# Attention, soft mixture of experts and MLP in one kernel: the dispatch sums spread behind the dispatch products, and a new order of the tail's steps

## The chip, the cores and the metric

One core of a Trainium2 chip runs the whole program. The metric is the time of one execution on the device in microseconds (us); the median of several executions is compared. The engines are named as in the profile: PE (matrix products; PEld is its loading of the stationary operand), DVE (vector), ACT (activations and copies), POOL (general), SP (issues the DMAs; SPq is its queue).

## The reference

Three layers follow each other, in float32. Eight batches with 8 heads, 576 rows and head size 64; keys and values are averaged over groups of 8 rows, so that each row attends to 72 pooled keys:

```python
k_p = k.reshape(B, H, Sp, pool, D).mean(axis=3); v_p = ...
attn = softmax(scale * q @ k_p.T); x = attn @ v_p          # 4608 x 512
logits = x @ phi                                           # 4608 x 32 slots (8 experts x 4)
d = exp(logits - logits.max(0)); d /= d.sum(0) + 1e-9
slot_input = d.T @ x                                       # dispatch
slot_out[e] = relu(slot_input[e] @ w1[e]) @ w2[e]
c = exp(logits - logits.max(1)); c /= c.sum(1) + 1e-9
x = c @ slot_out                                           # combine
out = (s * relu(x @ w_in) ** 2 + b) @ w_out
```

The maximum and the sum of d run over all 4608 rows, for each of the 32 slots. The kernel takes them batch by batch and merges the eight results.

## The kernel before

**The loop.** `for t in range(NT + 2)` goes over 36 tiles of 128 rows; a pair of batches (pr) has 9 tiles. A table (LOOP, FIRST) says in which order the steps of the pipeline are issued in each turn. For tile t: A transposes q (PE, L353; copied by ACT, L355), B forms the scores (PE, L383; DVE takes maximum and difference, L390 and L393), C takes the exponential on ACT (L397), its sum and reciprocal on DVE (L401 to L404) and the product P on POOL (L421), D transposes P (PE, L434 and L435; ACT copies to PT, L440 and L441), E forms the logits transposed (PE, L457 and L464; ACT copies to LT, L469), F turns them back (PE, L480) and DVE adds four partial sums into L (L482). "r" takes one step of each running dispatch, "p" one step of the preparation of a next pair (kv_transpose L264 and others).

**A dispatch.** When F has done the last tile of batch b_, a generator `dispatch(b_)` is started; each `next` issues the instructions up to its next `yield`. Its steps, in order: maximum of L over the rows (md, L538); the maximum over the partitions by a transposition on PE and a DVE reduction (L545, L547); its spreading over the partitions by a product (L550) with a DVE copy into m_all (L551); the difference dd (DVE, L554); its exponential (ACT, L556); then

- zd, the sum of dd over j (DVE, L559), its sum over the partitions spread to all partitions by a product with ones (PE, L563), and the copy of that into z_all (ACT, L564);
- the dispatch products of dd with the tiles P (PE, L572 and L577) into two banks, copied by ACT to `at` (L581);
- sums of four blocks by products with sel4 (PE, L591), copied to `a` (ACT L595; for the last batch DVE L597, multiplied by m_all);
- products with the pooled values vps (PE, L601), copied by DVE into si_all (L611); for the last batch DVE adds si_sum and writes the slot inputs siz (L613).

Batches 0 to 5 (b_ < B - 2) are dispatched inside the loop, with a `yield` between zd and L563. Batches 6 and 7 are dispatched in the tail.

**The tail.** The string TAIL (L21) is a list of steps that are issued in that order after the loop: F, E, C, D for one of the last five tiles, "6" and "7" one step of the dispatch of batch 6 or 7, "m" one step of merge_1 (maximum, si and z of the first six batches: L496 to L498, then L501 and L502, then L504 to L508), M2 (L515 to L517), M3 (L521 to L526) and M4 (L531, L532) the merging with batches 6 and 7, W products that have no use but to be run, X0 to X2 the closing of a tile pool and `extra`, which opens new slots for weights in its place and lets SP issue loads into them. "G4" is D for the last tile with its two copies on DVE in place of ACT.

**After the tail.** The weights w1 and w2 come as 32 loads of 1 MB, each into a slot (tiles ring, raw, x, and one called brief). PE multiplies them in a fixed order (L933 for w1, L941 for w2); after each, its slot is free and `pump` issues the next load in the list, in order, on the SP queue. The fifth load used, `brief`, can only be issued when the tail's pools are closed (actx.close()); the load behind it in the queue is the first of w_in, which needs a slot of `raw`, and so the sixth product's end. Beside these products the DVE and ACT steps of `combine` run, and PE transposes (L892) their results. From about 285 us on (L1067) the last layer runs on PE.

**Banks.** All products other than the scores use `bank()`, one pool of four tiles in rotation (ps_w): whoever asks for a tile waits until the one that was asked for four requests earlier has been read.

Of the kernel before, what the change touches and what calls it, by code (L numbers as in the profile page):

```python
# [14 lines left out]
ALU = mybir.AluOpType  # L15
AX = mybir.AxisListType
# [1 line left out]

OPS = "o0 a0 o0 a1 b0 b1 h0 g0 o1 h1 o1 g1"
WIPOS, WOPOS = 22, 25  # L20
TAIL = "F0 6 C4 X0 D2 6 X1 E2 6 m 6 6 F2 D3 G4 6 m E4 F4 X2 7 W3 7 W2 7 7 7 6 6 7 6 m M2 M3 7 7 M4 7"  # L21
BUSY = (2, 0)
CUT = 1

# [32 lines left out]
def kernel(  # L57
# [14 lines left out]
    nc = tc.nc  # L72
    B, H, SEQ, D = q.shape
    KP = SEQ // 8
    NPR = B // 2
    E, DM, F = w1.shape
# [12 lines left out]
    one = cpool.tile([128, 1], F32, name="one")  # L89
# [6 lines left out]
    z_all = cpool.tile([128, B, 32], F32, name="z_all")  # L96
# [81 lines left out]
    W1, W2 = ([[(w, e, hf) for e in range(EG * g, EG * g + EG) for hf in range(2)] for g in range(2)] for w in ("w1", "w2"))  # L178
# [36 lines left out]
    def bank():  # L215
        return ps_w.tile([128, 512], F32, tag="w", name="w")
# [206 lines left out]
    def place(t):  # L423


        jj = t % 9
        return (0, True) if jj == 0 else ((jj - 1) % 2, jj % 2 == 0)

    def st_D(t, copy=nc.scalar.copy):
        Pf = P_t[t].rearrange("p h k -> p (h k)")  # L430
        x, last = place(t)
        pa, pb = bank(), bank()
        for c in range(4):
            nc.tensor.transpose(out=pa[:, 128 * c:128 * c + 128], in_=Pf[:, 128 * c:128 * c + 128], identity=ident)  # L434
        nc.tensor.transpose(out=pb[0:64, 0:128], in_=Pf[:, 512:576], identity=ident)  # L435
        if x == 0:
            PT_t[t // 9] = apc.tile([128, 5, 256], F32, tag="PT", name="PT", bufs=2)
        PT = PT_t[t // 9]
        r = slice(128 * x, 128 * x + 128)
        copy(out=PT[:, 0:4, r], in_=pa.rearrange("p (c x) -> p c x", c=4))  # L440
        copy(out=PT[0:64, 4, r], in_=pb[0:64, 0:128])  # L441
        if last:
            PT2_t[t] = PT

# [89 lines left out]
    def dispatch(b_):  # L534
        pr, bb = divmod(b_, 2)
        Lb = L_t[pr][:, 6 * bb:6 * bb + 5, :]
        md = ap2.tile([128, 32], F32, tag="md", name="md")
        nc.vector.tensor_reduce(out=md, in_=Lb.rearrange("p j s -> p s j"), axis=AX.X, op=ALU.max)  # L538
        yield
        if b_ < B - 2:  # L540
            yield


        ps = bank()
        nc.tensor.transpose(out=ps[0:32, 0:128], in_=md, identity=ident)  # L545
        mc = md[0:32, 0:1]
        nc.vector.tensor_reduce(out=mc, in_=ps[0:32, 0:128], axis=AX.X, op=ALU.max)  # L547
        yield
        ps = bank()
        nc.tensor.matmul(out=ps[:, 0:32], lhsT=mc.to_broadcast([32, 128]), rhs=ident[0:32, 0:32], start=True, stop=True)  # L550
        nc.vector.tensor_copy(out=m_all[:, b_, :], in_=ps[:, 0:32])  # L551
        yield
        dd = ap2.tile([128, 5, 32], F32, tag="dd", name="dd")
        nc.vector.tensor_tensor(out=dd, in0=Lb, in1=m_all[:, b_, :].unsqueeze(1).to_broadcast([128, 5, 32]), op=ALU.subtract)  # L554
        yield
        nc.scalar.activation(out=dd, in_=dd, func=ACTF.Exp)  # L556
        yield
        zd = ap2.tile([128, 32], F32, tag="zd", name="zd")
        nc.vector.tensor_reduce(out=zd, in_=dd.rearrange("p j s -> p s j"), axis=AX.X, op=ALU.add)  # L559
        if b_ < B - 2:  # L560
            yield
        ps = bank()
        nc.tensor.matmul(out=ps[:, 0:32], lhsT=one.to_broadcast([128, 128]), rhs=zd, start=True, stop=True)  # L563
        nc.scalar.copy(out=z_all[:, b_, :], in_=ps[:, 0:32])  # L564
        t0 = 9 * pr + 1 + 4 * bb
        pure = [(dd[:, (1 if bb == 0 else 0) + j, :], P_t[t0 + j]) for j in range(4)]
        dl, Pm = dd[:, 0 if bb == 0 else 4, :], P_t[9 * pr]
        at = ap2.tile([128, PQ], F32, tag="at", name="at", bufs=1)
        pss = [bank(), bank()]
        for x in range(2):  # L570
            for g, (dj, P) in enumerate(pure):
                nc.tensor.matmul(  # L572
                    out=pss[x][32 * g:32 * g + 32, 0:288], lhsT=dj, rhs=P[:, 4 * x:4 * x + 4, :], start=True, stop=False
                )

            for g in range(4):
                nc.tensor.matmul(  # L577
                    out=pss[x][32 * g:32 * g + 32, 72 * g:72 * g + 72], lhsT=dl, rhs=Pm[:, 4 * x + g, :], start=False, stop=True
                )
        for x in range(2):  # L580
            nc.scalar.copy(out=at[:, 288 * x:288 * x + 288], in_=pss[x][:, 0:288])  # L581
        yield
        if b_ >= B - 2:
            yield
        for j in range(4):
            P_t.pop(t0 + j)
        if bb == 1:
            P_t.pop(9 * pr)
        ps = bank()
        for h in range(8):  # L590
            nc.tensor.matmul(out=ps[0:72, 32 * h:32 * h + 32], lhsT=at[:, 72 * h:72 * h + 72], rhs=sel4, start=True, stop=True)  # L591
        a = ap2.tile([72, 8, 32], F32, tag="a", name="a", bufs=1)
        av = ps[0:72, 0:256].rearrange("p (h s) -> p h s", h=8)
        if b_ < B - 1:
            nc.scalar.copy(out=a, in_=av)  # L595
        else:
            nc.vector.tensor_tensor(out=a, in0=av, in1=m_all[0:72, b_].unsqueeze(1).to_broadcast([72, 8, 32]), op=ALU.mult)  # L597
        yield
        ps = bank()
        for hp in range(4):  # L600
            nc.tensor.matmul(  # L601
                out=ps[:, 64 * hp:64 * hp + 64],
                lhsT=vps_t[pr][:, 4 * bb + hp, :],
                rhs=a[:, 2 * hp:2 * hp + 2, :],
                start=True, stop=True,
            )
        pv = ps[:, 0:256].rearrange("p (c t s) -> p c t s", c=4, t=2)
        for h2 in range(2):
            r = slice(64 * h2, 64 * h2 + 64)
            if b_ < B - 1:  # L610
                nc.vector.tensor_copy(out=si_all[r, b_], in_=pv[r, :, h2, :])  # L611
            else:
                nc.vector.tensor_tensor(  # L613
                    out=siz[r].rearrange("p (e r) -> p e r", r=132)[:, :, 0:128].rearrange("p e (c s) -> p e c s", s=32)[:, :, :, 0:4],
                    in0=pv[r, :, h2, :].rearrange("p c (e j) -> p e c j", j=4),
                    in1=si_sum[r].rearrange("p c (e j) -> p e c j", j=4),
                    op=ALU.add,
                )
# [119 lines left out]
    n0 = NT - 5  # L738

    def warm(n):  # L740
        ps = bank()
        for _ in range(n):
            nc.tensor.matmul(out=ps[:, 0:128], lhsT=ident, rhs=ident, start=True, stop=True)

    def step(gen, n=1):
        for _ in range(n):
            next(gen, None)
# [4 lines left out]
    cmb = [combine(pr) for pr in range(NPR)]  # L752
    siz = None
    for op in TAIL.split():
        if op[0] in "FECDG":
            t = n0 + int(op[1])
            if op[0] == "G":
                st_D(t, nc.vector.tensor_copy)
            else:
                {"F": st_F, "E": st_E, "C": st_C, "D": st_D}[op[0]](t)  # L760
        elif op[0] == "M":
            (merge_2, merge_3, merge_4)[int(op[1]) - 2]()
        elif op[0] == "W":
            warm(int(op[1:]))
        elif op[0] == "c":
            step(cmb[int(op[1])])
        elif op[0] == "X":
            (bctx, sctx, cctx)[int(op[1])].close()
            x_ = extra(XR[1 + int(op[1])], op[1] == "2")
            siz = siz if x_ is None else x_  # L770
        else:
            step(gens[op])
# [151 lines left out]
    for n_, key in enumerate(EORD):  # L924
# [3 lines left out]
        if w_ == "w1":  # L928
            for n in range(2):
                for c in range(2):  # L930
# [3 lines left out]
                        out=l1[g][n][32 * cg:32 * cg + 32, :],  # L934
                        lhsT=siz[:, 128 * e + 32 * kc:128 * e + 32 * kc + 32],
                        rhs=w[:, c, 512 * n:512 * n + 512],
                        start=(ge == 0), stop=(ge == EG - 1),
                    )
        else:
            for c in range(4):  # L940
                nc.tensor.matmul(  # L941
                    out=so_ps[32 * c:32 * c + 32, :],
                    lhsT=h1z[:, 4 * hf + c, 36 * ge + 16 - 4 * e:36 * ge + 48 - 4 * e],
                    rhs=w[:, c, :],
                    start=(e == 0 and hf == 0), stop=(e == E - 1 and hf == 1),
# [167 lines left out]
    for g, n in enumerate(GROUPS[:-1]):  # L1113
        m = GROUPS[g + 1]
# [9 lines left out]
    for i in range(len(steps)):  # L1124
# [18 lines left out]
        if t_wi:  # L1143
            f = min(t_wi)
            ps = ps_h.tile([128, 2, 512], F32, tag="h", name="h")
# [4 lines left out]
        if g == len(GROUPS) - 1:  # L1150
            if blk == 0 and fi == 0:

                ps = ps_h.tile([128, 2, 512], F32, tag="h", name="bias_ps")
# [5 lines left out]
            while bias:  # L1159
                p = part_of(*bias.popleft())  # L1160
# [31 lines left out]
```

## Time and profile before

| what | value |
|---|---|
| runs shown, median | 731.09 us (729.94 to 734.69, 3 runs) |
| profiled execution, its own time | 734.33 us |
| its span, first to last instruction | 732.2 us |
| PE busy | 662.1 us, 90% |
| DVE busy | 501.9 us, 69% |
| ACT busy | 412.0 us, 56% |
| POOL busy | 297.1 us, 41% |
| mean granted clock of PE | 0.960 of full |

Read: the profiled execution was slower than the median of the runs by 3.2 us, and its span leaves 2.1 us around it. A busy share is a mean over stages. Up to about 204 us the loop runs, from 204 to 228 us the tail, from 228 to 285 us the weights of the experts and the start of the last layer, and from there to the end PE is busy almost without a break.

### The profile page before, as it was taken

The page shows a single profiled execution, that of the slowest core. Times are in us where ns is not written, and L with a number is a line of the kernel's source. Part 1 is how long each engine was busy: PE and PEld are TensorE (multiplying, and loading weights), DVE is VectorE, ACT ScalarE, POOL GpSimd, SP SyncE. Part 2 cuts the span into 40 slices and gives each one's busy share as a digit, 9 for nine tenths or more (in the row PEclk, how much of TensorE's full clock was granted, in tenths as well). Part 3 has the DMA queues.
Part 4 walks back from the last instruction along what each step waited for, and adds up shares of the span by engine and source line. Part 5 has one row for each costly group of instructions (what it writes and reads, how often), then busy time and mean ns, then how long its engine had stood idle before and what let it go on. Part 6 is the DMA issues. An engine that isn't in the chain of part 4 may idle for free.

```text
span 732.2 us, 11203 instructions
## 1 busy us (share of the span) xinstructions
PE 662.1 (90%) x4294; PEld 517.9 (71%) x4294; DVE 501.9 (69%) x806; ACT 412.0 (56%) x713; POOL 297.1 (41%) x221
## 2 busy tenths in 40 slices
PE   4676879788877987999999999999999999999997
PEld 3565757577653325778888887878888888888885
DVE  6869778657667268788767687889655766456543
ACT  3454656466431435778665666666666666555552
POOL 3647556533210025356322443346331433799100
PEclk9886999999997998999999999999999999999999
DMA  8996455444384993101111011031100000123322
GB/s 298 375 328 209 174 168 181 172 173 164 125 288 175 379 358 123 58 0 58 59 57 59 8 61 48 1 115 59 58 1 0 1 1 1 44 95 95 100 100 87
DMA packets 41317, 88.87 MB, mean 121 GB/s; under 512 B 6960, under 2 KB 15152, under 8 KB 41264
## 3 DMA queue, kind: packets, MB, share of 16 engines
q1 hardware_dynamic: 41264, 88.16, 34.6%
q8 instruction: 34, 0.56, 0.3%
q14 instruction: 19, 0.16, 0.1%
HBM read 78.71 MB, written 9.44 MB: 120 GB/s over the span
## 4 chain that ended last, share of the span: by engine, by line
PE 75%; DVE 15%; ACT 4%; POOL 2%; issue 2%; DMA 1%; SPq 1%; DVEq 0%; ACTq 0%; POOLq 0%
PE o L1067 52%; PE h L1010 4%; PE sc L383 2%; PE l L933 2%; DVE sm L401 2%; DVE S L393 2%; PE so_ps L941 2%; DVE mx L390 2%; PE w L572 2%; PE w L434 1%; DMA ring<-in_v_dram 1%; ACT S L397 1%; PE w L591 1%; PE w L457 1%; PE ct L892 1%
## 5 line engine op out<-in xcount | busy, mean ns | idle before, releaser
L1067 PE MATMUL o<-whi,gh 128*128 128x512 f32 x576 | 229.1, 398 | 2.5 <-DVE gh L1037 2.5
L1067 PE MATMUL o<-whi,gl 128*128 128x512 f32 x576 | 225.2, 392 | 1.0 <-DVE gl L1038 1.0
L1067 PE MATMUL o<-wlo,gh 128*128 128x512 f32 x576 | 225.2, 391 | 0.0
L1019 ACT ACTIVATE r<-h 128x768 f32<-128x768 f32 x95 | 77.3, 813 | 151.8 <-PE h L1010 148.0
L1038 DVE TENSOR_TENSOR gl<-r,gh 128x768 fp32r<-128x768 f32 (+1 forms) x97 | 114.4, 1181 | 63.3 <-ACT gh L1027 62.9
L1080 DVE SCALAR_TENSOR_TENSOR part<-o,sb_t,part 128x512 f32<-128x512 f32 x144 | 99.6, 743 | 50.4 <-PE o L1067 47.8
L1067 PEld LDWEIGHTS o<-wlo,gh 128*128 128x128 f32 x576 | 108.5, 188 | 24.0
L1067 PEld LDWEIGHTS o<-whi,gh 128*128 128x128 f32 x576 | 108.4, 188 | 23.8 <-issue 5.6
L1067 PEld LDWEIGHTS o<-whi,gl 128*128 128x128 f32 x576 | 108.6, 189 | 21.7 <-DVE gl L1038 3.1
L825 POOL TENSOR_TENSOR fr<-fr,xp 128x512 f32<-128x512 f32 x28 | 41.1, 1467 | 182.4 <-ACT fr L824 160.3
L1020 ACT ACTIVATE r<-r 128x768 f32<-128x768 f32 x95 | 80.5, 847 | 3.0
L1027 ACT CAST gh<-r 128x768 fp32r<-128x768 f32 x95 | 79.4, 836 | 2.4
L421 POOL TENSOR_TENSOR P<-S,rs 128x576 f32<-128x576 f32 x32 | 37.3, 1166 | 89.7 <-DVE rs L404 54.9
L1161 POOL TENSOR_TENSOR part<-part,wsum 128x512 f32<-128x512 f32 x36 | 53.3, 1518 | 10.5 <-ACT wsum L1155 10.5
L1010 PE MATMUL h<-cT,S 128*128 128x384 f32 x192 | 48.8, 336 | 0.5 <-DVE S L853 0.5
L826 POOL TENSOR_TENSOR th<-th,fr 128x512 f32<-128x512 f32 x28 | 43.0, 1537 | 2.2
L383 PE MATMUL sc<-kb,qT 128*128 128x144 f32 x256 | 42.0, 313 | 0.0
L1010 PEld LDWEIGHTS h<-cT,S 128*128 128x128 f32 x192 | 35.9, 188 | 8.1 <-DVE S L853 0.7
L401 DVE TENSOR_REDUCE sm<-S 128x8 f32<-128x576 f32 x36 | 27.0, 750 | 21.2 <-ACT S L397 21.0
L390 DVE TENSOR_REDUCE mx<-sc 128x8 f32<-128x576 f32 x36 | 26.4, 732 | 18.7 <-PE sc L383 15.3
L383 PEld LDWEIGHTS sc<-kb,qT 128*128 128x128 f32 x256 | 37.8, 212 | 0.4 <-ACT qT L355 0.2
L397 ACT ACTIVATE S<-S 128x576 f32<-128x576 f32 x36 | 24.6, 682 | 22.1 <-DVE S L393 22.0
(212 smaller groups left out, 913.1 us busy)
## 6 DMA issues: line engine op xcount, KB each, us to landing
ring<-in_moe_w_dram SPq DMA_DIRECT2D x14, 1024.0 KB, 7.3
x<-in_moe_w_dram SPq DMA_DIRECT2D x13, 1024.0 KB, 10.5
raw<-in_moe_w_in_dram SPq DMA_DIRECT2D x8, 1024.0 KB, 5.5
raw<-in_moe_w_out_dram SPq DMA_DIRECT2D x8, 1024.0 KB, 4.8
out_dram<-part SPq DMA_DIRECT2D x32, 256.0 KB, 2.5
ring<-in_q_dram SPq DMA_DIRECT2D x7, 1024.0 KB, 9.5
ring<-in_v_dram SPq DMA_DIRECT2D x9, 768.0 KB, 10.0
ring<-in_k_dram SPq DMA_DIRECT2D x7, 768.0 KB, 7.0
```

The lines of the kernel that those rows point to most:

```text
L383: nc.tensor.matmul(out=sc[:, i // 2, 2 * KP * (i % 2):2 * KP * (i % 2) + 2 * KP], lhsT=qT[:, i, :], rhs=kb[:, H * bb + 4 * (j % 2) + i, :] ...
L401: nc.vector.tensor_reduce(out=sm, in_=S, axis=AX.X, op=ALU.add)
L825: nc.gpsimd.tensor_tensor(out=fr, in0=fr, in1=xp, op=ALU.mult)
L826: nc.gpsimd.tensor_tensor(out=th if dst is None else dst, in0=th, in1=fr, op=ALU.add)
L1010: nc.tensor.matmul(out=h[x][:, 0:384] if i == 0 else h[:, x, 0:384], lhsT=Sw_t[f], rhs=cT(c, 384), start=True, stop=True)
L1019: nc.scalar.activation(out=r, in_=h[:, :, 0:384], func=ACTF.Relu)
L1020: nc.scalar.activation(out=r, in_=r, func=ACTF.Square)
L1027: nc.scalar.copy(out=gh_t[i], in_=r)
L1038: nc.vector.tensor_tensor(out=gl[:, x], in0=r[:, x], in1=gh[:, x].bitcast(F32), op=ALU.subtract)
L1067: nc.tensor.matmul(out=o_t[tt], lhsT=l[:, x, 128 * c:128 * c + 128], rhs=r, start=(fi == 0 and n == 0), stop=(fi == GROUPS[g] - 1 and n == 2),
L1080: nc.vector.scalar_tensor_tensor(out=p, in0=o_t[tt], scalar=sb_t[:, 0:1], in1=p, op0=ALU.mult, op1=ALU.add)
L1161: nc.gpsimd.tensor_tensor(out=p, in0=p, in1=wsum, op=ALU.add)
```

## The change

In `dispatch`, the sum over the partitions (product L563 and its copy L564) is taken out of the place in front of the dispatch products and put behind them. For batches 0 to 5 zd stays in its own step and the spreading comes one step later, at the head of the step that begins with the sel4 products. For batches 6 and 7 zd, too, moves behind the dispatch products, into the step that did nothing before; for batch 7 the copy is made by DVE. The string TAIL is new: D for the last tile makes its copies on ACT (D4 in place of G4, whose code goes), the last step of merge_1 stands before F4, M2 directly behind the exponential of batch 7, and M3 before the last step of batch 6.

```diff
-TAIL = "F0 6 C4 X0 D2 6 X1 E2 6 m 6 6 F2 D3 G4 6 m E4 F4 X2 7 W3 7 W2 7 7 7 6 6 7 6 m M2 M3 7 7 M4 7"
+TAIL = "F0 6 C4 X0 D2 6 X1 E2 6 m 6 6 F2 D3 m D4 6 E4 6 m F4 X2 7 W3 7 W2 7 7 7 M2 6 7 7 M3 6 7 M4 7"
...
         zd = ap2.tile([128, 32], F32, tag="zd", name="zd")
-        nc.vector.tensor_reduce(out=zd, in_=dd.rearrange("p j s -> p s j"), axis=AX.X, op=ALU.add)
+
+        def z_sum():
+            nc.vector.tensor_reduce(out=zd, in_=dd.rearrange("p j s -> p s j"), axis=AX.X, op=ALU.add)
+
+        def z_spread(copy):
+            ps = bank()
+            nc.tensor.matmul(out=ps[:, 0:32], lhsT=one.to_broadcast([128, 128]), rhs=zd, start=True, stop=True)
+            copy(out=z_all[:, b_, :], in_=ps[:, 0:32])
+
         if b_ < B - 2:
+            z_sum()
             yield
-        ps = bank()
-        nc.tensor.matmul(out=ps[:, 0:32], lhsT=one.to_broadcast([128, 128]), rhs=zd, start=True, stop=True)
-        nc.scalar.copy(out=z_all[:, b_, :], in_=ps[:, 0:32])
         t0 = 9 * pr + 1 + 4 * bb
...
             nc.scalar.copy(out=at[:, 288 * x:288 * x + 288], in_=pss[x][:, 0:288])
         yield
-        if b_ >= B - 2:
+        if b_ < B - 2:
+            z_spread(nc.scalar.copy)
+        else:
+            z_sum()
+            z_spread(nc.scalar.copy if b_ < B - 1 else nc.vector.tensor_copy)
             yield
```

On PE, inside the loop at the dispatch of batch 1, before: the product with ones (zd, one) stands between the scores and the dispatch products (P, dd).

```order
L383 MATMUL sc<-kb_124,qT 128x144 x4
L563 MATMUL w<-zd,one 128x32
L572 MATMUL w<-P_2_104,dd 32x288 x2
L572 MATMUL w<-P_3_105,dd 32x288 x2
L577 MATMUL w<-Pm,dd 32x72 x4
L572 MATMUL w<-P_2_104,dd 32x288 x2
L572 MATMUL w<-P_3_105,dd 32x288 x2
L577 MATMUL w<-Pm,dd 32x72 x4
L353 MATMUL w<-ident,qm 128x128 x4
```

The same place on PE now, from the end of the dispatch products (here L583) on: the product with ones (now L565) stands behind the steps A, E and D and in front of the products with sel4 (now L601).

```order
L583 MATMUL w<-Pm,dd 32x72 x4
L353 MATMUL w<-ident,qm 128x128 x4
L457 MATMUL w<-PT,vpf 32x256 x4
L464 MATMUL w<-PT,vpf 32x64 x4
L434 MATMUL w<-ident,P_0_102 128x128 x4
L435 MATMUL w<-ident,P_0_102 64x128
L565 MATMUL w<-zd,one 128x32
L601 MATMUL w<-sel_62,at 72x32 x8
L383 MATMUL sc<-kb_124,qT 128x144 x4
```

So the dispatch products come directly behind the scores, and PE has four other steps before it asks for zd.

On DVE, at the end of the tail, before: what stands between the copies of batch 6 into si_all and the multiplication `a` of batch 7 (L597), namely the last step of merge_1 (L504 to L508), M2 and M3.

```order
L611 COPY si_all<-w 64x128 x2
L504 TENSOR_TENSOR z_all<-z_all,m_all 128x192
L506 TENSOR_REDUCE zt<-z_all 128x32
L507 COPY z_all<-zt 128x32
L508 COPY m_all<-mt 128x32
L515 TENSOR_REDUCE mt<-m_all 128x32
L516 TENSOR_TENSOR m_all<-m_all,mt 128x96
L521 TENSOR_TENSOR z_all<-z_all,m_all 128x96
L523 TENSOR_REDUCE zt<-z_all 128x32
L524 TENSOR_SCALAR zt<-zt 128x32
L525 RECIPROCAL zt<-zt 128x32
L526 TENSOR_TENSOR m_all<-m_all,zt 128x96
```

The same place on DVE now, from the difference dd of batch 7 on to the multiplication `a` (now L607):

```order
L554 TENSOR_TENSOR dd<-L_75,m_all 128x160
L515 TENSOR_REDUCE mt<-m_all 128x32
L516 TENSOR_TENSOR m_all<-m_all,mt 128x96
L561 TENSOR_REDUCE zd<-dd 128x32
L566 COPY z_all<-w 128x32
L521 TENSOR_TENSOR z_all<-z_all,m_all 128x96
L523 TENSOR_REDUCE zt<-z_all 128x32
L524 TENSOR_SCALAR zt<-zt 128x32
L525 RECIPROCAL zt<-zt 128x32
L526 TENSOR_TENSOR m_all<-m_all,zt 128x96
L621 COPY si_all<-w 64x128 x2
L607 TENSOR_TENSOR a<-w,m_all 72x256
```

M2 has moved ahead of zd, the step L504 to L508 is gone from here (it now stands before F4), and the copies into si_all follow M3.

## Rows read from the trace of the kernel before

**Rows 1.** Waits of PE from 75 to 204 us: total, times, longest.
```profile
PE w L563 <- DVE zd L559: 9.3, 4, 3.0
```

**Rows 2.** Timeline of PE, L563: start, duration, ..., [idle before <- releaser]; batches 1, 2, 4, 5.
```profile
104.84 0.61 PE L563 MATMUL w<-zd,one 128*128 128x32 f32 x2 [3.00 <-DVE zd L559]
131.63 0.45 PE L563 MATMUL w<-zd,one 128*128 128x32 f32 x2 [2.35 <-DVE zd L559]
177.61 0.38 PE L563 MATMUL w<-zd,one 128*128 128x32 f32 x2 [1.31 <-DVE zd L559]
195.37 0.38 PE L563 MATMUL w<-zd,one 128*128 128x32 f32 x2 [2.60 <-DVE zd L559]
```

**Rows 3.** Timeline of ACT: exponentials and copies of batches 1 and 5, and in the tail.
```profile
102.27 0.34 ACT L556 ACTIVATE dd<-dd 128x160 f32<-128x160 f32 x1 [2.03 <-DVE dd L554]
103.20 0.59 ACT L440 COPY PT<-w 128x512 f32<-128x512 f32 x1
192.80 0.34 ACT L556 ACTIVATE dd<-dd 128x160 f32<-128x160 f32 x1 [1.09 <-DVE dd L554]
211.31 0.19 ACT L564 COPY z_all<-w 128x32 f32<-128x32 f32 x1 [2.04 <-PE w L563]
```

**Rows 4.** Busy time by stretch: length, PE, PEld, DVE, ACT, POOL, granted clock, DMA share, GB/s.
```profile
104.00:108.00 4.00, 3.16 (x35) 1.80 (x36) 2.08 (x5) 1.08 (x4) 3.11 (x3) 0.57 0.95 302
132.00:135.00 3.00, 3.00 (x35) 1.52 (x34) 0.91 (x2) 0.88 (x3) 1.93 (x2) 0.50 0.63 239
196.70:200.00 3.30, 3.30 (x40) 2.05 (x29) 1.18 (x4) 1.89 (x5) 0.18 (x1) 0.50 0.00 0
224.00:234.00 10.00, 7.59 (x36) 3.35 (x40) 8.00 (x25) 1.33 (x3) 0.00 (x0) 0.50 0.43 154
```

**Rows 5.** Timeline of PE in the tail and behind it.
```profile
210.90 0.38 PE L563 MATMUL w<-zd,one 128*128 128x32 f32 x2 [1.18 <-DVE zd L559]
217.88 0.41 PE L563 MATMUL w<-zd,one 128*128 128x32 f32 x2 [0.31 <-DVE zd L559]
218.22 0.69 PE L572 MATMUL w<-P,dd 128*32 128x288 f32 x8
219.58 1.10 PE L601 MATMUL w<-a,vps 72*128 72x64 f32 x8
225.46 1.97 PE L601 MATMUL w<-a,vps 72*128 72x64 f32 x8 [3.77 <-DVE a L597]
228.37 4.49 PE L933 MATMUL l<-ring,siz 128*32 128x512 f32 x20 [0.94 <-DVE siz L613]
...
234.69 1.04 PE L933 MATMUL l<-brief,siz 128*32 128x512 f32 x8
```

**Rows 6.** Timeline of DVE at the tail's end.
```profile
221.32 0.36 DVE L504 TENSOR_TENSOR z_all<-z_all,m_all 128x192 f32<-128x192 f32 x1
...
223.43 0.26 DVE L521 TENSOR_TENSOR z_all<-z_all,m_all 128x96 f32<-128x96 f32 x1 [0.35 <-ACT m_all L517]
...
224.99 0.42 DVE L597 TENSOR_TENSOR a<-w,m_all 72x256 f32<-72x256 f32 x1
```

**Rows 7.** Timeline of the SP queue, loads of weights.
```profile
214.80 1.51 SPq L136 DMA_DIRECT2D x<-in_moe_w_dram  x1
216.35 0.89 SPq L136 DMA_DIRECT2D x<-in_moe_w_dram  x1
...
227.50 0.37 SPq L136 DMA_DIRECT2D brief<-in_moe_w_dram  x1
236.67 0.37 SPq L136 DMA_DIRECT2D raw<-in_moe_w_in_dram  x1
```

**Rows 8.** These two x loads and the brief load: size, us from issue to landing.
```profile
x<-in_moe_w_dram SPq DMA_DIRECT2D x1, 1024.0 KB, 10.5
x<-in_moe_w_dram SPq DMA_DIRECT2D x1, 1024.0 KB, 11.4
...
brief<-in_moe_w_dram SPq DMA_DIRECT2D x1, 1024.0 KB, 4.8
```

More of the change, by code (lines that the diff above doesn't have):

```diff
@@ L427, in place, with st_D @@
         return (0, True) if jj == 0 else ((jj - 1) % 2, jj % 2 == 0)
-    def st_D(t, copy=nc.scalar.copy):
+    def st_D(t):
         Pf = P_t[t].rearrange("p h k -> p (h k)")
@@ L439, in st_D @@
         r = slice(128 * x, 128 * x + 128)
-        copy(out=PT[:, 0:4, r], in_=pa.rearrange("p (c x) -> p c x", c=4))
-        copy(out=PT[0:64, 4, r], in_=pb[0:64, 0:128])
+        nc.scalar.copy(out=PT[:, 0:4, r], in_=pa.rearrange("p (c x) -> p c x", c=4))
+        nc.scalar.copy(out=PT[0:64, 4, r], in_=pb[0:64, 0:128])
         if last:
@@ L754 @@
     for op in TAIL.split():
[L755 to L760, printed above, removed]
+        if op[0] in "FECD":
+            {"F": st_F, "E": st_E, "C": st_C, "D": st_D}[op[0]](n0 + int(op[1]))
         elif op[0] == "M":
```

## The prediction

> **What bounds the kernel now.** I read the waits of PE first, then the timelines of PE and ACT around them, then the chain from the tail into the weights. The reader is to see three things.
>
> In the loop PE stands still in front of one instruction, the product with ones (L563). It waits 9.3 us in four stretches for zd [rows 1], those of batches 1, 2, 4 and 5: 3.00, 2.35, 1.31 and 2.60 us [rows 2]; batches 0 and 3 show none. Behind it on PE the dispatch products are queued, and they don't read zd; they read dd, whose exponential ended earlier: at batch 1 at 102.27 + 0.34 = 102.61, while PE came free at 104.84 - 3.00 = 101.84 and zd let it go at 104.84 [rows 2, 3]. DVE makes zd only after the sums of the next tile. So the wait is one of order, not of data. Nothing in the loop runs against an outer clock that I can find, so a time won there is kept until another engine stands in the way.
>
> In the tail PE waits for zd again, 1.18 us for batch 6 and 0.31 for batch 7, and then 3.77 us for `a` of batch 7 [rows 5], because DVE does the rest of merge_1, M2 and M3 between the copies of batch 6 and that multiplication: from 221.32 to 224.99 [rows 6]. During that idle time the granted clock falls to 0.50, the 1.2 GHz level, and it is there from 224 to 234 [rows 4]. The last products (L601) take 1.97 us, the same kind before them 1.10 [rows 5].
>
> Behind the tail, the weights of w1 and w2 are multiplied, and new loads are issued as slots come free. `brief` is issued at 227.50, when the tail's last products are over, and the next load only at 236.67, after the sixth weight is used [rows 7]. From there on loads and products follow one another at a pace that the start decides, and the last layer follows on them. I take it that a shift at `brief` is a shift of the end.
>
> **The change part by part.** *Loop, dispatch products ahead of the product with ones.* At batch 1 the wait is 3.00; the products must still wait for the exponential, 102.61 - 101.84 = 0.77. Their second bank was asked for last by D, whose copy to PT ends at 103.20 + 0.59 = 103.79 [rows 3]; the products take 1.36 us in the tail (218.22 to 219.58 [rows 5]), so the first half would be through at about 103.3, and another 0.5 is waited. That leaves 3.00 - 0.77 - 0.5 = 1.7. At batches 2 and 4 I count the whole wait, 2.35 and 1.31. At batch 5 the exponential ends at 192.80 + 0.34 = 193.14 against 195.37 - 2.60 = 192.77 [rows 2, 3], so 2.60 - 0.37 = 2.2. The sum is 1.7 + 2.35 + 1.3 + 2.2 = 7.6 us (rounded up). The product itself (0.38 to 0.61 us [rows 2]) is not saved, it comes back in front of the products with sel4; there zd has long been made, so it waits for nothing. Behind it on PE the sel4 products and the next scores are queued; their delay is the same 0.4 us that the dispatch products are spared.
>
> The loop's term has bounds. Above: PE ran at half clock behind three of these waits: 3.16 us of PE work at 0.57 after batch 1, 3.00 at 0.50 after batch 2, 3.30 at 0.50 after batch 5 [rows 4]. With the waits gone that work could run at the full 2.4 GHz, worth 3.16 x 0.43 + 3.00 / 2 + 3.30 / 2 = 4.5 us more, 12.1 in all. Below: another engine may be late next; then I count only the 1.7 of batch 1. I take 7.6, the value of the waits' own rows, and leave the clock out, since PE keeps other waits.
>
> *Tail, up to the first weight.* For batch 6 PE no longer waits for zd: 1.2 us. The copies of the last D go from DVE to ACT, where 2.04 us were idle before 211.31 [rows 3]; two such copies are 0.85 at most, judged by 0.59 for the larger, so they are covered; without that cover they would cost that 0.85. For batch 7 wait and product stood ahead of the dispatch products, 218.22 - 217.57 = 0.65, as the wait of 0.31 began at 217.57 [rows 5]. Then the main piece: from the end of the dispatch products, about 219.58, to `a` at 224.99 there were 5.4 us [rows 5, 6]. Now there stand the product with ones (0.3), its copy (0.2, as ACT's), M3 (224.99 - 223.43 = 1.56 [rows 6]) and the two copies into si_all (from 220.68, where the products L601 end, to 221.32 [rows 5, 6], 0.64): 2.7. M2 and the end of merge_1 lie beside PE's work earlier, where DVE is waiting. That saves 2.7. Products with sel4 for batch 7 end near the same moment and don't bind. With PE's wait gone, the last L601 should take 1.10 in place of 1.97: 0.9. Sum 1.2 + 0.65 + 2.7 + 0.9 = 5.4 us at the first weight product, so 228.37 becomes 223.0, and the issue of `brief` 222.1, counted in the time of before.
>
> *Tail, up to brief.* The first weights now run at the full clock: four of them at 1.04 us each (as the one of `brief` [rows 5]) are through at 227.1, where before they took until 234.69 [rows 5]. But `brief` is not there yet. It stands in the queue behind x loads that land at 214.80 + 10.5 = 225.3 and 216.35 + 11.4 = 227.75 [rows 7, 8]. That load rate doesn't depend on the change. At their spacing of 2.45 us `brief` lands at 230.2. PE waits some 3 us for it, a new wait that replaces the one removed. The gain at that point, and from there to the end, is 234.69 - 230.2 = 4.5 us. Bounds: it lands with the load ahead of it, 227.75 (gain 6.9), or it takes the whole 4.8 us that it took alone [rows 8] behind it, 232.55 (gain 2.1). I take 4.5, the value from the two queued loads, because it is queued as they are.
>
> The sum: 7.6 + 4.5 = 12.1 us. The profiled execution took 734.33, so its like would take 722.2. That execution was 3.2 above the median of the runs; against the median of 731.09 the forecast is 719.0.
>
> **The rivals.** *The clock comes back.* As above, three half-clock stretches stand right behind removed waits [rows 4]; if all go, the gain is 12.1 + 4.5 = 16.6, and the time 731.09 - 16.6 = 714.5. Against it: the new wait at `brief`, and waits in the loop that stay. The Trainium skill, "TensorE: Matmul & The Clock Gate", section "HAM oscillation — how this bites in real kernels", says that a kernel whose products are short bursts between waits keeps falling back to the low clock and pays for it each time; by that rule the loop's falls would go with their waits, and a new one could come at `brief`. By that rule, the trace agrees as far as [rows 4] go, where each of the three stretches stands behind a wait for zd.
>
> *Another engine is late in the loop.* The removed wait is replaced by the next one, as DVE's sums and POOL's products follow one another too. For it: at batch 1 PT's copy at 103.79 is 1.95 behind PE's free moment. Then the loop gives 1.7 and the sum is 1.7 + 4.5 = 6.2: 724.9.
>
> *Brief lands late.* If it needs the full 4.8 us behind the last x load, the tail gives 2.1 and the sum is 7.6 + 2.1 = 9.7: 721.4.
>
> *Slower.* Place: the banks of the dispatch products. They are asked for earlier, when ACT has not read the tiles that hold them, and ACT now has a copy for D more and is served in order. Price: each dispatch waits for ACT what it waited for DVE before. The point from which it decides is (7.6 + 4.5) / 8 = 1.5 us per dispatch; at 2.0 us in each of eight the kernel loses 16.0 - 12.1 = 3.9: 735.0. For it speaks the same PT copy, against it that only batch 1 shows it so late and that ACT is the least busy of the three engines here.
>
> **How the numbers follow.** Forecast 0.54, clock back 0.18, another engine 0.15, brief late 0.10, slower 0.03. A measurement of this kernel can tell about 1% from no change, 7.3 us, that is below 723.8 or above 738.4; 735.0 is still within 1%, but such waits would not stop at 2.0 exactly, and I give 0.02 of its 0.03 to slower. Faster: nearly all of the forecast (0.52), the clock (0.18), most of brief late (0.09) and a little of the third (0.03), together 0.82. Slower 0.02, the rest, 0.16, within 1%. The range goes from both upper bounds, 731.09 - 12.1 - 6.9 = 712.1, to both lower ones, 1.7 + 2.1 = 3.8 us and so 727.3; I give it as 712.0 to 727.0.
>
> **What would show it.** Right: PE's waits for zd are gone in the loop, the dispatch products follow the exponential or their bank; the tail from the exponential of batch 7 to the first weight is some 4 us shorter; PE has a wait of up to 3 us for `brief`; the stretch from the loop's start to the tail's is 7 to 12 us shorter, and the last layer as long as before. Wrong in the loop: waits of the same size in front of the scores, the transpositions of D or DVE's sums. Wrong in the tail: PE still waits for `a`, or the load behind `brief` is issued less than 2 us earlier, counted from the tail's start.

## The result and the profile after

| what | before | changed |
|---|---|---|
| runs beside each other, median | 730.67 us (729.94 to 734.69, 4 runs) | 722.06 us (719.37 to 727.48, 4 runs) |
| ratio | | 0.9876, 95% interval 0.9837 to 0.9915 |
| profiled execution, its own time | 734.33 us | 724.16 us |
| its span | 732.2 us | 722.0 us |
| mean granted clock of PE | 0.960 | 0.956 |

The change was run in two more series of six (e3_all and e6_change below): 0.9866 and 0.9859. A gain in us is given, here and below, as the ratio gives it: 1 less the ratio, times the median of the kernel before. One slow execution (733.7 us, in e1_loop) is in the median shown there and not in the ratio. So the change saves 9 to 10 us (9.1, 9.8 and 10.3) of the 12.1 forecast.

The waits of PE from 75 to 204 us of the changed kernel (total, times, longest), which answer to [rows 1]:

```profile
PE w L578 <- ACT dd L556: 1.3, 2, 0.9
...
PE w L601 <- ACT LT L469: 1.2, 2, 0.8
...
PE w L434 <- POOL P L421: 0.6, 1, 0.6
PE w L565 <- DVE L L482: 0.5, 1, 0.5
...
PE w L578 <- ACT PT L440: 0.3, 1, 0.3
```

zd, 9.3 us before, is gone from the list. L578 are now the dispatch products, L565 the product with ones, L601 the products with sel4. The timeline of PE at batches 1, 2 and 5, which answers to [rows 2]:

```profile
103.63 0.69 PE L578 MATMUL w<-P,dd 128*32 128x288 f32 x8 [0.88 <-ACT dd L556]
...
104.76 0.69 PE L578 MATMUL w<-P,dd 128*32 128x288 f32 x8 [0.31 <-ACT PT L440]
...
107.51 0.31 PE L565 MATMUL w<-zd,one 128*128 128x32 f32 x2
108.19 1.23 PE L601 MATMUL w<-sel,at 128*72 128x32 f32 x16 [0.37 <-ACT LT L469]
...
131.44 0.41 PE L565 MATMUL w<-zd,one 128*128 128x32 f32 x2 [0.51 <-DVE L L482]
131.98 1.80 PE L601 MATMUL w<-sel,at 128*72 128x32 f32 x16
...
192.41 1.23 PE L601 MATMUL w<-sel,at 128*72 128x32 f32 x16 [0.79 <-ACT LT L469]
193.47 1.92 PE L383 MATMUL sc<-kb,qT 128*128 128x144 f32 x8
```

The dispatch products at batch 1 wait for the exponential and then for D's copy to PT, as foreseen. What is new are small waits: one of D's transpositions (L434) for POOL's P, 0.6 us, and those of L565 and L601, which name neither zd nor `at`. L565 doesn't read L, nor L601 LT; counted by the rotation of four, L565 of batch 2 asks for the bank of F, which F's sum (L482) is still reading, and L601 for the bank of E, which E's copy (L469) is still reading.

The clock by stretch (columns as in [rows 4]):

```profile
104.00:108.00 4.00, 3.51 (x59) 2.13 (x50) 2.95 (x7) 3.48 (x10) 2.43 (x3) 1.00 1.10 354
132.00:135.00 3.00, 3.00 (x22) 3.00 (x23) 1.23 (x4) 1.02 (x4) 1.85 (x2) 0.57 0.07 27
194.00:204.00 10.00, 9.80 (x56) 7.55 (x59) 7.01 (x17) 3.53 (x10) 1.76 (x2) 0.50 0.56 204
214.70:221.10 6.40, 5.46 (x28) 2.79 (x32) 4.72 (x15) 0.89 (x2) 0.00 (x0) 0.50 0.90 338
```

The low clock behind batch 1 is gone. Behind batches 2 and 5 it is there again, now behind the waits of 0.51 and 0.79 for a bank: most of the scores L383 at 193.47 run at 1.2 GHz. It is there too from 143 to 146 (0.50), behind a wait for DVE that the kernel before has as well, of the same length and without a fall of the clock (1.00 from 144 to 150 there):

```profile
141.44 0.37 PE L550 MATMUL w<-ident,md 32*128 32x32 f32 x2 [1.59 <-DVE md L547]
```

The length of the wait ahead doesn't tell whether the clock falls. In e3_all, a second profile of the same kernel, the waits of batches 2 and 5 are as long, a wait of 2.69 us for POOL stands at 150, and the clock is at the 2.4 GHz level all the way from 90 to 212 us:

```profile
134.19 0.41 PE L565 MATMUL w<-zd,one 128*128 128x32 f32 x2 [0.51 <-DVE L L482]
150.48 0.55 PE L264 MATMUL w<-ident,vp 128*128 128x128 f32 x3 [2.69 <-POOL vp L251]
193.41 1.23 PE L601 MATMUL w<-sel,at 128*72 128x32 f32 x16 [0.79 <-ACT LT L469]
...
90.00:212.00 122.00, 105.03 (x1302) 85.15 (x1299) 93.71 (x210) 71.23 (x181) 51.83 (x43) 1.00 0.54 193
```

The kernel before has that wait of 2.69 us too, and there the clock is low behind it (152 to 156 us); behind its wait of 1.31 for zd at batch 4 it is not (1.00 from 177 to 182).

In the tail the low clock is there once more. The rows on PE answer to [rows 5]:

```profile
211.74 1.08 PE L611 MATMUL w<-a,vps 72*128 72x64 f32 x8
212.66 1.18 PE L601 MATMUL w<-sel,at 128*72 128x32 f32 x16
214.70 1.97 PE L611 MATMUL w<-a,vps 72*128 72x64 f32 x8 [0.86 <-DVE a L607]
217.61 5.37 PE L939 MATMUL l<-ring,siz 128*32 128x512 f32 x32 [0.94 <-DVE siz L623]
223.50 1.06 PE L939 MATMUL l<-brief,siz 128*32 128x512 f32 x8 [0.52 <-DMA brief<-in_moe_w_dram]
```

The wait for `a` fell from 3.77 to 0.86. DVE's rows (against [rows 6]) show M3 beginning at 212.24, right behind the copy of z (L566), and ending at 213.69 (L526). PE comes free at 213.84, so the merge is over by then; what PE still waits for are the two copies into si_all that stand in front of `a` on DVE, and `a` itself:

```profile
211.95 0.19 DVE L566 COPY z_all<-w 128x32 f32<-128x32 f32 x1 [1.46 <-PE w L565]
212.24 0.26 DVE L521 TENSOR_TENSOR z_all<-z_all,m_all 128x96 f32<-128x96 f32 x1
...
213.43 0.26 DVE L526 TENSOR_TENSOR m_all<-m_all,zt 128x96 f32<-128x96 f32 x1
213.61 0.58 DVE L621 COPY si_all<-w 64x128 f32<-64x128 f32 x2
214.22 0.42 DVE L607 TENSOR_TENSOR a<-w,m_all 72x256 f32<-72x256 f32 x1
```

The loads on the SP queue (against [rows 7, 8]); `brief` took 6.7 us from issue to landing, 4.8 before:

```profile
216.74 0.37 SPq L136 DMA_DIRECT2D brief<-in_moe_w_dram  x1
225.50 0.37 SPq L136 DMA_DIRECT2D raw<-in_moe_w_in_dram  x1
```

Five markers cut the profiled execution into stretches: the first product with sel4 of batch 0, that of batch 5, the product with `brief`, the first product of the last layer (L1073 here, L1067 before), and the end. The three profiles of the change are this one and those of e3_all and e6_change.

| stretch, us | before | changed | e3_all | e6_change | gain forecast |
|---|---|---|---|---|---|
| start to sel4 of batch 0 | 86.59 | 87.47 | 90.22 | 89.06 | 0 |
| to sel4 of batch 5 | 113.11 | 104.94 | 103.19 | 105.95 | 7.6 |
| to `brief` | 34.99 | 31.09 | 30.35 | 32.21 | 4.5 |
| to the last layer | 49.46 | 49.47 | 49.49 | 49.45 | 0 |
| to the end | 448.05 | 449.03 | 448.05 | 447.83 | 0 |

The loop gained 8.2, 9.9 and 7.2 us, the tail 3.9, 4.6 and 2.8. The start, where no wait was removed, lost 0.9, 3.6 and 2.5 of it. Between `brief` and the last layer nothing changed, to 0.04 us.

### The profile page after: what moved, and what is told of

It reads as the page before. It is cut to its first block, busy times and chain, and to the rows that moved or that the text cites. A ratio compares the mean times of both kernels' runs of the same rounds, so it can differ in the third digit from the quotient of the medians.

```text
span 722.0 us, 11198 instructions
## 1 busy us (share of the span) xinstructions
PE 665.4 (92%) x4294; PEld 522.2 (72%) x4294; DVE 499.0 (69%) x805; ACT 411.4 (57%) x714; POOL 297.3 (41%) x221
## 4 chain that ended last, share of the span: by engine, by line
PE 73%; DVE 16%; ACT 4%; DMA 2%; POOL 2%; issue 2%; SPq 1%; DVEq 0%; POOLq 0%; ACTq 0%
PE o L1073 52%; PE h L1016 4%; PE sc L383 3%; DVE S L393 2%; DVE mx L390 2%; DVE sm L401 2%; PE l L939 2%; DMA ring<-in_v_dram 1%; PE w L434 1%; ACT S L397 1%; PE w L601 1%; PE so_ps L947 1%; DMA brief<-in_moe_w_dram 1%; PE w L578 1%; PE ct L898 1%
## 5 line engine op out<-in xcount | busy, mean ns | idle before, releaser
L1073 PE MATMUL o<-whi,gh 128*128 128x512 f32 x576 | 229.4, 399 | 2.5 <-DVE gh L1043 2.5
L1073 PE MATMUL o<-whi,gl 128*128 128x512 f32 x576 | 225.5, 392 | 0.8 <-DVE gl L1044 0.7
L1073 PE MATMUL o<-wlo,gh 128*128 128x512 f32 x576 | 225.6, 392 | 0.0
L1073 PEld LDWEIGHTS o<-whi,gh 128*128 128x128 f32 x576 | 108.8, 189 | 24.1 <-issue 5.8
L1073 PEld LDWEIGHTS o<-wlo,gh 128*128 128x128 f32 x576 | 108.7, 189 | 24.1
L1073 PEld LDWEIGHTS o<-whi,gl 128*128 128x128 f32 x576 | 108.8, 189 | 21.6 <-DVE gl L1044 2.8
L383 PE MATMUL sc<-kb,qT 128*128 128x144 f32 x256 | 44.3, 325 | 0.0
L383 PEld LDWEIGHTS sc<-kb,qT 128*128 128x128 f32 x256 | 40.0, 223 | 0.4 <-ACT qT L355 0.2
```

The costliest lines, as they stand in the source:

```text
L383: nc.tensor.matmul(out=sc[:, i // 2, 2 * KP * (i % 2):2 * KP * (i % 2) + 2 * KP], lhsT=qT[:, i, :], rhs=kb[:, H * bb + 4 * (j % 2) + i, :] ...
L1073: nc.tensor.matmul(out=o_t[tt], lhsT=l[:, x, 128 * c:128 * c + 128], rhs=r, start=(fi == 0 and n == 0), stop=(fi == GROUPS[g] - 1 and n == 2),
```

## The experiments

All were timed in five rounds beside the kernel before. Where a lost clock is given, it is worked out from each execution's span and mean granted clock, span x (1 - clock), and averaged over the executions of a kernel.

**The two parts alone.** e1_loop does only the loop's part, here in outline:

```diff
 # batches 0 to 5, in the kernel before
-        ps = bank(); matmul(ps, one, zd); copy to z_all
         ... dispatch products, copies to at, yield
+        ps = bank(); matmul(ps, one, zd); copy to z_all
```

> Only the loop's part of the change: batches 0 to 5 spread zd behind the dispatch products, the tail is as before. Theory (the wait for zd in the loop is worth about its length): 6 to 7 us faster than the kernel before, PE's waits for zd in the loop gone. Rival (another engine or the clock takes the wait's place): less than 3 us.

Measured: 725.6 us against 732.53, ratio 0.9909 (0.9874 to 0.9944), -6.7 us. In its profile the stretch from sel4 of batch 0 to that of batch 5 is 104.78, a gain of 8.3, and that to `brief` 33.56, a gain of 1.4, though its tail is the old one: by that much one profile's tail can differ by itself.

e2_tail does only the tail's: the new TAIL, D of the last tile on ACT, and for batches 6 and 7 the product with ones behind the dispatch products.

> Only the tail's part: batches 6 and 7 and the new string of steps, the loop is as before. Theory: 4 to 5 us faster than the kernel before, `brief` is issued 5 us earlier counted from the tail's start, and PE waits for it. Rival (the loads of weights set the end whatever the tail does): within 2 us of the kernel before.

Measured: 727.2 us, ratio 0.9934 (0.9908 to 0.9959), -4.8 us. Its loop still waits as before, and as long (113.10); the stretch to `brief` is 29.26, a gain of 5.7. `brief` is issued 4.65 us earlier, counted from sel4 of batch 5, but the wait of PE for it that was expected isn't there. PE's wait in the loop:

```profile
PE w L565 <- DVE zd L561: 9.3, 4, 3.0
```

e3_all is the change again, on the same chip.

> The whole change once more, beside its two parts on the same chip. Theory: its gain is the sum of the two parts, 10 to 12 us. Rival (the parts compete for the same idle time, or the clock gives one back): 2 us or more below the sum.

Measured: 722.14 us, ratio 0.9866 (0.9836 to 0.9896), -9.8 us, just under the 10 to 12 expected. The parts alone add up to 11.5. The missing 1.7 is within the intervals (1.9 to 2.6 us each way), so that the parts disturb each other isn't shown.

**Wait or place?** e4_zd_early leaves the product with ones ahead of the dispatch products, and lets DVE make zd one step earlier, right behind the exponential:

```diff
         nc.scalar.activation(out=dd, in_=dd, func=ACTF.Exp)
-        yield
+        if b_ >= B - 2:
+            yield
         zd = ...
         nc.vector.tensor_reduce(out=zd, in_=dd..., op=ALU.add)
         if b_ < B - 2:
             yield
+            yield
```

> The kernel before, with zd of batches 0 to 5 summed by DVE right behind the exponential and ahead of the next tile's sums; the product with ones stays ahead of the dispatch products. Theory (what costs is the wait for zd, not the product's place): PE's wait for zd falls from 9.3 us below 4 and the kernel is 3 to 6 us faster. Rival (the product's place in front costs): no faster than 2 us, though the wait is shorter.

Measured: 727.41 us, ratio 0.9932 (0.9907 to 0.9958), -5.0 us. From 75 to 204 us:

```profile
PE w L565 <- DVE zd L560: 2.1, 2, 1.2
...
PE w L565 <- DVE L L482: 1.6, 1, 1.6
```

From sel4 of batch 0 to that of batch 5 it takes 104.32 us, no more than e1_loop's 104.78, and the intervals of the two ratios overlap. So most of the loop's gain, if not all, is to be had with the product where it was; what cost was the wait of what is queued behind it.

**Are the new waits those of the banks' rotation?** e5_zbank takes one request for a bank out of each dispatch: the product with ones goes into free columns of the bank of the sel4 products.

```diff
-        def z_spread(copy):
-            ps = bank()
+        def z_spread(copy, ps=None):
+            ps = bank()[:, 256:288] if ps is None else ps[:, 256:288]
...
-            z_spread(nc.scalar.copy)
+            ps = bank()
+            z_spread(nc.scalar.copy, ps)
...
-        ps = bank()
+        ps = bank() if ps is None else ps
```

> The change, with the loop's product with ones (L565) put into free columns of the bank that the products with sel4 take behind it, so that each dispatch of the loop asks for one bank less. Theory: what the change lost in the loop is lost to the rotation of the banks; L565 asked for a bank that DVE (F) still read, the products L601 for one that ACT (E) still read, and the clock fell behind these waits. Then both waits (1.3 and 1.2 us in the changed kernel's profile) go or move and the time is 1 to 4 us below the change run beside it (e6_change). Rival: the sums of DVE and the copies of ACT are late whatever bank is asked for; the waits stand in front of another product and the time is within 1 us of e6_change.

e6_change is the change, run beside it.

> The change itself, as the partner of the other three. Both theories: 9 to 10 us below the kernel before, ratio 0.9865, with PE's wait for brief between 0.5 and 1.7 us.

Measured: e5_zbank 729.9 us, ratio 0.9967 (0.9946 to 0.9987); e6_change 723.33 us, 0.9859 (0.9826 to 0.9893), without the wait for `brief` that was expected of it. Neither theory had it 6.6 us above the change. Its waits from 75 to 204 us tell why:

```profile
PE w L603 <- ACT z_all L566: 5.7, 6, 1.5
```

The sel4 products (L603 there) write other columns of the same tile and now wait until ACT has copied z out of it, in each dispatch. The edit took the waits for LT away and put six for z in their place: it says nothing on the rotation. It does say what such a wait costs. PE waited 5.7 us more for this; the clock lost 30.4 us on average against 25.6, and the time rose by 6.6.

e9_zpss avoids that: the product goes into free columns of the second bank of the dispatch products, whose copy the sel4 products wait for in any case.

```diff
-        def z_spread(copy):
-            ps = bank()
+        def z_spread(copy, ps=None):
+            ps = bank() if ps is None else ps[:, 288:320]
...
-            z_spread(nc.scalar.copy)
+            z_spread(nc.scalar.copy, pss[1])
```

> The change, with the loop's product with ones (L565) put into free columns of the second bank of the dispatch products in front of it (PSUM tile pss[1], columns 288 to 319). The products with sel4 keep a bank of their own, so they have nothing new to wait for; L565 itself waits for the copy of pss to at, which the products with sel4 right behind it wait for in any case. Theory (rotation of the banks): the waits of L565 for F's sums (0.5) and of L601 for LT (1.2 in e6_change) go, with the falls of the clock behind them, and the time is 1 to 4 us below the change, ratio to before 0.980 to 0.985. Rival: the waits only change their product, the ratio is that of the change, 0.986 or more.

Measured: 721.92 us, ratio 0.9877 (0.9849 to 0.9905), the change's. From 75 to 204 us:

```profile
PE w L601 <- ACT LT L469: 1.2, 2, 0.8
...
PE w L435 <- DVE L L482: 0.6, 1, 0.6
```

The time is the rival's. The 0.5 of L565 stands in front of L435 now, and that of L601 stayed. But the edit frees no bank: pss[1] is now read last when z is copied, behind the steps that PE does in between, so that only three banks rotate there. Counted so, L435 asks for F's bank and L601 for E's, which are the two waits in the rows. Whether a bank more would remove them no run tells.

**The merge steps of the tail.** e7_merge_late puts them back behind the dispatch products of batch 7:

```diff
-... m D4 6 E4 6 m F4 X2 7 W3 7 W2 7 7 7 M2 6 7 7 M3 6 7 M4 7
+... m D4 6 E4 6 F4 X2 7 W3 7 W2 7 7 7 6 7 7 6 m M2 M3 7 M4 7
```

> The change, with the merge steps (the third step of merge_1, M2 and M3) put back behind the dispatch products of batch 7. It tells the prediction's 2.7 us for the merge steps in the tail. Theory: a for batch 7 comes about 2.7 us later, the first weight product too, and of this what brief had been late with is absorbed (0.5 to 1.7), so 1 to 2.5 us above e6_change. Rival: the tail is bound by the loads alone; brief is issued when its place comes free and not by the first weight, the time is within 0.5 us of e6_change and PE's wait for brief is gone.

Measured: 725.21 us, ratio 0.9904 (0.9877 to 0.9931), 1.9 us above e6_change by the medians. Its PE in the tail:

```profile
217.91 1.97 PE L611 MATMUL w<-a,vps 72*128 72x64 f32 x8 [3.76 <-DVE a L607]
220.82 5.64 PE L939 MATMUL l<-ring,siz 128*32 128x512 f32 x32 [0.94 <-DVE siz L623]
226.28 1.04 PE L939 MATMUL l<-brief,siz 128*32 128x512 f32 x8
```

The wait for `a` is back, 3.76 in place of 0.86: the order of the merge is worth 2.9 us at `a`, about 2 at the end by the medians. PE doesn't wait for `brief` here. The intervals of the two ratios overlap a little, so the time alone doesn't show the 2; the wait for `a` is 0.86 in all three profiles of the change.

**What bounds the tail's end?** e8_brief6 loads the seventh weight used, not the fifth, into the place of `brief` (BRIEF = 6 in place of 4).

> The change, with the seventh weight in place of the fifth loaded into the place of brief (BRIEF = 6). Theory: PE's wait for brief (0.5 to 1.7 us) goes, PE's products run on at the full clock, and the time is 0.5 to 2 us below e6_change. Rival: the queue of loads sets the pace behind brief, the wait moves to a later load and the time is within 0.5 us of e6_change; or it is longer, since the place of brief is handed back two weights later.

Measured: 722.35 us, ratio 0.9872 (0.9839 to 0.9906). By the medians that is 1.0 below e6_change, by the ratios 1 above; the two are not told apart, and so neither are theory and rival. e6_change itself shows no wait for `brief` in its profile, so there was little to win.

e10_warm puts products that have no use into PE's two waits at the end of the tail:

```diff
-... 7 7 M3 6 7 M4 7
+... 7 7 M3 6 7 W8 M4 7 W8
```

> The change, with eight products of ident with itself into a bank of their own in front of M4 and eight behind the last step of batch 7, that is in PE's waits for a (0.86 us) and for siz (0.94 us) in the tail; they add nothing to the output. Theory: PE keeps 2.4 GHz through the first weights, whose first 32 products then take 4.2 in place of 5.4 us, but brief lands when it did, so PE's wait for brief grows by what the weights gain and the time is within 1 us of the change (ratio 0.984 to 0.988). Rival: the first weights set the pace, and the time falls by 1 to 2 us, without a longer wait for brief.

Measured: 724.24 us, ratio 0.9893 (0.9869 to 0.9916), 0.9 us above e6_change by the medians, the ratio a little above the expected 0.984 to 0.988 (e9 to e12 ran on another chip than e6_change, so the ratios are the better measure).

```profile
215.68 2.03 PE L753 MATMUL w<-ident 128*128 128x128 f32 x16
217.55 1.00 PE L611 MATMUL w<-a,vps 72*128 72x64 f32 x8
...
220.50 3.64 PE L939 MATMUL l<-ring,siz 128*32 128x512 f32 x32
224.92 1.06 PE L939 MATMUL l<-brief,siz 128*32 128x512 f32 x8 [0.79 <-DMA brief<-in_moe_w_dram]
```

The clock holds (the first weights take 3.64 in place of 5.37 us, vps 1.00 in place of 1.97), but eight such products (two records each) take 2.03 us for a wait of 0.86, and PE waits 0.79 for `brief` behind the faster weights. e11_warm_brief6 has both edits:

> Both edits of the tail: the products of e10_warm, and the seventh weight in place of the fifth in the place of brief (e8_brief6). Theory: with brief used two weights later the faster products are not given back, and the time is 1 to 3 us below the change (ratio 0.982 to 0.985). Rival: the loads behind it set the pace, the wait moves to brief at its new place or to a later load, and the time is within 1 us of the change.

Measured: 721.08 us, ratio 0.9858 (0.983 to 0.9887). The ratio is that of the change (0.9859 to 0.9876 in its three series), and PE waits 0.50 us for `brief` at its new place: the rival's, though by the medians it is 1 to 2 us below.

**Together.** e12_all_edits has e9's bank, three useless products in place of eight, and BRIEF = 7.

> The change with three edits together, to see whether they beat it: the loop's product with ones in the second bank of the dispatch products (e9_zpss), three products of ident in each of PE's two waits of the tail where e10_warm had eight (eight took 2.0 us each for waits of 0.9), and the eighth weight in the place of brief (BRIEF = 7). Theory: the tail keeps 2.4 GHz without being lengthened, PE doesn't wait for brief, and the time is 1 to 3 us below the change, ratio 0.982 to 0.985. Rival: after the last product of the tail the loads set the pace whatever PE does, from the issue of the first load behind brief to the first product of the output stage it is 47.5 us or more as in every run so far, and the ratio is that of the change, 0.986 to 0.988.

Measured: 718.79 us against 731.5, ratio 0.9817 (0.978 to 0.9853), -13.4 us, just beyond the theory's 0.982. The rival's stretch, from the issue of the first load behind `brief` to the last layer, is 50.37 us, so its floor of 47.5 held and the time fell all the same. It is the lowest of all, and its median 3.6 us below the mean of the 16 executions of the change (722.4). The intervals overlap, and the two were not timed side by side, so that it beats the change is likely and not shown. In its tail:

```profile
210.69 0.91 PE L753 MATMUL w<-ident 128*128 128x128 f32 x6
211.72 1.10 PE L611 MATMUL w<-a,vps 72*128 72x64 f32 x8
212.66 0.89 PE L753 MATMUL w<-ident 128*128 128x128 f32 x6
213.76 3.64 PE L939 MATMUL l<-ring,siz 128*32 128x512 f32 x32 [0.22 <-PE w L753]
...
221.75 0.44 PE L898 MATMUL ct<-ident,cs 128*128 128x128 f32 x2 [1.77 <-DVE cs L893]
```

The three products fill the waits almost exactly. PE no longer waits for `brief`; it waits 1.77 us for DVE's step of `combine` (cs) instead. The clock lost 20.0 us on average in its six executions, 25.6 in e6_change; which of the three edits did that isn't told apart. The profiles don't tell it either: the loop's 103.29 is e3_all's and e8_brief6's too (103.19, 103.15), and from sel4 of batch 5 to the last layer it takes 79.21, e8_brief6 77.48 and e9_zpss 77.95.

## Why the prediction was right

The time, 722.06, lies in the range, and the direction was right. The forecast of 719.0 was 3 us too low.

*The loop's term, 7.6.* Right, in its closeness partly by luck. From sel4 to sel4 the profile of the change gives 2.6 at batch 1 (23.35 to 20.72; forecast 1.7), 2.9 at batch 2 (2.35), 1.1 at batch 4 (1.3), 1.9 at batch 5 (2.2) and loses 0.3 at batch 3 (0): 8.2 in all. The two waits that were to remain at batch 1, 0.77 for the exponential and 0.5 for PT, are there with 0.88 and 0.31. e1_loop alone gave 6.7 at the end. At batch 1 the low clock went with the wait (0.57 to 1.00), which the term doesn't count; at batch 3 the clock is low twice (132 to 135 and 143 to 146), which it doesn't count either. In e3_all, whose clock stays high through the loop, the loop gave 9.9; in e6_change, where it is low from 133 to 144 us and from 195 on, 7.2.

*The clock left out.* Right on average. The rival that it comes back (0.18) fell: it lost 26.9, 24.8 and 25.6 us on average in the three series of the change, and 26.9, 27.1 and 26.5 in the three series of the kernel before that stood beside the experiments. About 1 of the 4.5 us came back. That rival's argument, that each fall stood behind a wait for zd and would go with it, didn't carry. The fall behind batch 1 is gone in all three profiles of the change. The others come and go with the execution: in the first profile they stand behind waits of 0.51 and 0.79, in e3_all the same waits have none. What decides it stays open. The Trainium skill, "TensorE: Matmul & The Clock Gate", section "A second HAM failure mode: psum-queue depth-cycling", describes a kernel whose products cycle through banks and pause briefly between groups, so that the clock goes up and down. By that rule, the trace agrees with the falls at 132 to 135 and from 194; e3_all, with the same pauses and the clock at 1.00 from 90 to 212, shows that such pauses alone don't bring it down.

*Tail to the first weight, 5.4.* From sel4 of batch 5 to the first weight product the three profiles take 3.5, 5.5 and 2.0 us less than the 28.67 before; the 5.5 is e3_all's, whose clock is high up to 212 us. One term failed, the 0.9 for vps at the full clock: the wait for `a` shrank to 0.86, and the clock fell in it all the same (at 214.3 us), so the last L611 takes 1.97 as before (1.97 in e3_all, 1.82 in e6_change; 1.10 only in e8_brief6). The merge order is right in kind: 2.7 was forecast, 2.9 is what e7_merge_late has more of the wait for `a`.

*Tail to `brief`, 4.5.* Right in size for the changed kernel (3.9, 4.6 and 2.8 by the stretches; e2_tail gave 4.8 at the end), by another way than described. The queue went as forecast in two of the three profiles: `brief` landed 3.9, 2.4 and 2.5 us behind the last x load (forecast 2.45), which is 6.7, 8.1 and 5.7 us behind its issue (forecast 8.1). But the weights ahead of it ran mostly at half clock (5.37 us for four, not 4.2). So PE waited for it 0.5 us, 1.7 in e3_all and nothing in e6_change, not 3. The rival that it lands late (0.10), 4.8 us behind the last x load, fell. That a shift at `brief` is a shift of the end held to 0.04 us up to the last layer.

*Where 2 to 3 us went.* The sum of 12.1 held for the stretches that it speaks of: 12.1, 14.6 and 9.9 in the three profiles. The median of the time doesn't show all of it. In the profiles, 0.9, 3.6 and 2.5 us were lost ahead of sel4 of batch 0, and 1.0 in the last layer of one of them. The clock has a part in that: it is low from 84 to 88 us in e3_all, from 82 to 86 in e6_change, and up to 280 us in the changed kernel; e3_all also waits 1.6 us for its loads of q at the start, the kernel before 0.4. That the change costs something at the start isn't seen: the eight profiles that have its loop take 84.6 (e1_loop) to 90.2 us there, 87.5 on average, the two with the old loop (before and e2_tail) 87.3. What is left of the 2 to 3 us stays open; the one profile of the kernel before that the stretches are measured against is itself of an execution 3.2 us above the median.

*Another engine late (0.15), and slower by the banks (0.03).* Both mechanisms are there, and small: the waits for a bank are 0.3 to 0.8 us each, not 2.0 in every dispatch.

## To carry to other kernels

When an engine waits at an instruction, look whether what is queued behind it needs the same datum; if not, moving it behind that work is worth the wait, less the waits that come next in the queue, and these can be read from the trace ahead of the change. Making the datum earlier can do as much (e4_zd_early). A low clock behind the wait should not be counted as won: here it came back in some executions behind waits left over, and in others not, so one profile doesn't tell. Before two results share a bank, ask who has to wait until the other has been read.

## Not expected of the hardware

- Executions of the same kernel differ by the clock. In the six of e6_change the span goes from 715.0 us at a mean granted clock of 0.973 to 724.5 at 0.957; the lost clock goes from 19.3 to 31.2 us. One profile is therefore no measure of a difference below 1%.
- The clock fell behind short waits, 0.51 us at 131.44 and 0.79 at 192.41, and stayed at 1.2 GHz while PE was busy for 9.80 of the 10 us from 194 to 204. In e3_all it fell behind neither, nor behind a wait of 2.69.
- With three products that nobody reads in each of the tail's two waits, 0.9 us each time, the clock stayed at 2.4 GHz from the last vps products through the weights in e12_all_edits; with eight of them, 2.0 us, it did too (e10_warm, e11_warm_brief6). In the other eleven profiles it fell once between 211 and 224 us. The eight took longer than the wait that they filled.
- Products into one part of a bank's columns waited until ACT had read another part: 5.7 us in six dispatches (e5_zbank). The trace shows the wait, not whether the chip needs it.
